# Reciprocals of the attention denominators: GpSimd's power of minus one in place of VectorE's reciprocal

## The chip, the cores and the metric

The kernel runs on one core of a Trainium2 chip. The time is the device time of one execution in microseconds (us). The core has five engines with queues of their own, which meet only through semaphores: TensorE (PE) multiplies matrices, VectorE (DVE) and ScalarE (ACT) work on tiles in SBUF and PSUM, GpSimd (POOL) on tiles in SBUF, and SyncE (SP) issues the DMAs here. PEld in the profile is PE's weight load, which runs beside its products.

## The reference

One token block of S = 2048 rows and D = 512 columns goes through a layernorm, and then through two branches whose results are added to the input.

```python
xn  = layernorm(x)
# A: linear attention, H = 32 heads of 16 columns
phi = lambda t: where(t > 0, t + 1, exp(t)) + 1e-6
pq, pk = phi(q), phi(k)
kv  = einsum("bhsd,bhse->bhde", pk, v);  z = sum over s of pk
num = einsum("bhqd,bhde->bhqe", pq, kv)
den = einsum("bhqd,bhd->bhq", pq, z)[..., None] + 1e-6
A   = (num / den) @ wo
# B: gated feed-forward, F = 1792
B   = (silu(xn @ w_gate) * (xn @ w_up)) @ w_down
out = x + A + B
```

For each of the 2048 rows there are 32 denominators, one per head. The division by them is what the change touches.

## The kernel before

The rows are cut into NT = 16 tiles of 128 (the partitions). A small planner, `_Program`, takes operations in the order in which they are written, with the keys that they read and write. It gives each engine its own queue in that order, and puts a semaphore wait wherever an operation depends on one of another engine, or reads what an earlier one of its own engine wrote (PE excepted). So the order on every engine is that of the source, and an operation that waits holds back all that stands behind it on its engine.

The first 75 us do the layernorm, q, k and phi, the sum over k, and the feed-forward branch for the first 512 rows. The change is used after that.

**The F loop** (L1132, 14 chunks, `fc`) computes the feed-forward branch's hidden values for the other 1536 rows, in two halves `q`. Blocks of the product are combined so that seven products (`prod`, L846) take the place of eight, from sums of the weights that DVE forms (`w_sums`, L808, half of them in each chunk) and sums of the results (`u4`, L874, and `up22`, which writes the tile c, L879, both on DVE). POOL multiplies two of the four results of a chunk by the gate (`h22`, L883), DVE the two others (`h21`, L889). ACT does the gate (L868) and copies. Between the products `fill` puts matrix products of the first output tiles.

**The denominators** are worked off beside this, one tile `t` in each chunk 0 to 10 (`DIV`), in the order of the list `ORDER`, with two buffers each for `pz`, `den` and `rden`:

- `pz_mul` (L638, POOL): pq times z, 128x512, and a seventeenth column per head that holds 1e-6;
- `den_sum` (L644, DVE): the sum over the 17 columns of each head, which gives `den`, 128x32;
- `den_turn` (L650): `rden`, the reciprocals, 128x32;
- `pq_mul` (L654, POOL): pq times rden, spread over the 16 columns of a head;
- `turn` (L660, SP): a transposing DMA of pq into pk, from where PE reads it as weights for the output.

In a chunk the order is: `den_turn` after the two `u4`, then `up22` and `h22`, then `h21`, `w_sums`, `pq_mul` (which is also made to wait for the last weight sum), `turn`, `pz_mul` for the tile two further on (`pz_ahead`), and `den_sum` for the next chunk's tile. In chunks 9 and 10 POOL also scales half of M (L794), in 11 to 13 it copies parts of the down projection's weights (L998).

**The pair stage** (L1231) computes the output for the other 12 row tiles, in pairs, again with seven products for eight (`dprod`, L1083), and the attention's part (`attn`, L1089). DVE forms the sums of hidden values (`h_sum`, L1067), and the results (L1103, L1109, L1115). The five last denominators are worked off here (`DIV2`), one in each of the pairs 1 to 4 and the last one late in pair 4. There `den_sum`, `den_turn`, `pq_mul` and `turn` follow each other directly.

Of the kernel before, what the change touches and what calls it, by code (L numbers as in the profile page):

```python
# [7 lines left out]
ALU = mybir.AluOpType  # L8

P = 128  # L10
# [11 lines left out]
NH = D // DH  # L22
# [95 lines left out]
def bass_parallel_sum__linear_attn_block__swiglu_ffn__prompt_kernel(nc, A_x, A_wqkv, A_wo, B_x, B_w_gate, B_w_up, B_w_down, out):  # L118
    xin = A_x[0]
    oview = out[0]  # L120
    K = _Program()
    bf, f32 = dt.bfloat16, dt.float32

    with contextlib.ExitStack() as es:
        E = es.enter_context

        def sb(name, shape, dtype):
            return E(nc.sbuf_tensor(name, shape, dtype))
# [29 lines left out]
        den = sb("den", [P, 2, NH], f32)  # L158
        rden = sb("rden", [P, 2, NH], f32)
        out_sb = sb("out_sb", [P, 2, D], bf)  # L160
        ident = sb("ident", [P, P], bf)
        maskt = sb("maskt", [P, P], bf)
        eps5 = sb("eps5", [P, 1], f32)
        stats = sb("stats", [P, NT, 6], f32)
        mv = sb("mv", [P, NT, 2], f32)
        lnv = sb("lnv", [P, NT], f32)
# [99 lines left out]
        for t in range(4, 16):  # L266
            xload("sp", t)

        K.add("pool", lambda e: e.memset(eps5[:, :], 1e-5), w=[("eps5",)])
        K.add("pool", lambda e: e.memset(ident[:, :], 0.0), w=[("ident",)])  # L270
        K.add("pool", lambda e: e.affine_select(
            out=ident[:, :], in_=ident[:, :], compare_op=ALU.not_equal, fill=1.0,
            base=0, pattern=[[-1, P]], channel_multiplier=1), r=[("ident",)], w=[("ident",)])
# [373 lines left out]

        def den_turn(t):
            i = SLOT[t] % 2
            K.add("dve", lambda e: e.reciprocal(rden[:, i, :], den[:, i, :]), r=[("den", i)], w=[("rden", i)])  # L650

        def pq_mul(t, after=()):
            i = SLOT[t] % 2
# [10 lines left out]
        def divide(t):  # L664
            den_sum(t)
            den_turn(t)
            pq_mul(t)
            turn(t)
            pz_mul(t + 2)
# [462 lines left out]
        for fc in range(NFC):  # L1132
# [16 lines left out]
            if fc in DIV:  # L1149
                den_turn(DIV[fc])  # L1150
# [80 lines left out]
        for p in range(NP2 - 1):  # L1231
# [6 lines left out]
            if p == 0:  # L1238
                t_sum(3, 0)
                t_sum(3, 1)  # L1240
                h_sum(0, 2)
            else:
                copies(p, 0)
                if p > 1:
                    h_sum(p, 3)
                den_sum(t)
                den_turn(t)
                pq_mul(t)
                turn(t)
# [104 lines left out]
```

## Time and profile before

| | |
|---|---|
| median of 3 runs | 200.51 us (200.5 to 200.74) |
| profiled execution, its own time | 200.89 us |
| its span in the profile | 199.6 us |
| granted clock of TensorE | 1.00 |
| busy: PE, DVE, ACT, POOL | 98%, 85%, 77%, 61% |

The span runs from the first to the last instruction that the profile records. "Busy" counts instructions that run; PE's ends are modelled, since matrix products overlap. A row of a group names the line of the source, engine, operation, the tile written and the tiles read, shapes and count, then the busy time in us with the mean of one in ns, then the idle time of the engine just before them and what ended it. A line of the timeline gives start and length in us, and in brackets the idle time ahead of it with its releaser. The profile calls the tile c22 "c", p5 "p", and sil4 "zacc", the buffer that it lies in; hT, xn and pq also hold hidden values later on.

### The profile page before, as it was taken

Reading aid. Unit: us, or ns where it says so; the run is one execution under the profiler, and the core shown is the slowest. Engines: PE = TensorE matmul, PEld = TensorE weight load, DVE = VectorE, ACT = ScalarE, POOL = GpSimd, SP = SyncE. Lnnn points to the kernel's source line nnn. Section 1 sums busy time; section 2 is a strip of 40 time slices with the busy share of each in tenths; the row PEclk is TensorE's granted clock in tenths of the full one; section 3 lists DMA queues with packets and bytes.
Section 4 is the critical chain, followed back from the end, with each engine's and each line's share of the span. In section 5 each row is a group of like instructions: output and inputs, shape, how many; then the busy total and the mean of one; then the engine's idle time right before and its main releaser. Section 6 shows DMA issues by size and latency. Waiting matters only on the chain.

```text
span 199.6 us, 3566 instructions
## 1 busy us (share of the span) xinstructions
PE 195.1 (98%) x1193; PEld 114.8 (58%) x1207; DVE 170.5 (85%) x339; ACT 153.6 (77%) x308; POOL 122.3 (61%) x150
## 2 busy tenths in 40 slices
PE   8899999999999999999999999999999999999995
PEld 2344444444544445555555555555555888888884
DVE  2999998894797798988888998887799999998866
ACT  3799887749889988689898988888989968475200
POOL 3687876799995544787677666768877004413220
DMA  6943243289990000011111221000210012132223
GB/s 180 355 122 81 57 87 73 50 282 364 375 295 3 0 3 0 0 28 31 26 26 26 53 56 23 4 0 7 45 34 0 3 39 66 30 79 66 45 69 118
DMA packets 28899, 15.97 MB, mean 80 GB/s; under 512 B 17232, under 2 KB 28880, under 8 KB 28880
## 3 DMA queue, kind: packets, MB, share of 16 engines
q1 hardware_dynamic: 28320, 15.28, 27.3%
q10 hardware_dynamic: 560, 0.46, 0.7%
q8 instruction: 9, 0.15, 0.3%
q14 instruction: 10, 0.08, 0.1%
HBM read 9.70 MB, written 2.10 MB: 59 GB/s over the span
## 4 chain that ended last, share of the span: by engine, by line
PE 94%; DVE 2%; DMA 2%; issue 1%; ACT 0%; POOL 0%; SPq 0%
PE pb L846 32%; PE pb L1083 16%; PE pb L431 13%; PE pb L556 12%; PE pb L480 7%; PE pb L682 6%; PE pb L1089 5%; PE pb L686 2%; DMA x_sb<-in_A_x_dram 2%; PE pb L605 1%; PE pb L674 0%; DVE pq L470 0%; PE pb L398 0%; POOL ef L459 0%; DVE stats L298 0%
## 5 line engine op out<-in xcount | busy, mean ns | idle before, releaser
L654 POOL TENSOR_TENSOR pq<-pq,rden 128x512 bf16<-128x512 bf16 x16 | 16.9, 1056 | 36.7 <-DVE rden L650 23.1
L868 ACT ACTIVATE zacc<-pb,iw 128x384 bf16<-128x384 f32 x56 | 31.3, 590 | 5.9 <-PE pb L846 4.7
L431 PE MATMUL pb<-wqkv,xnT 128*128 128x512 bf16 x110 | 25.1, 379 | 0.2
L846 PE MATMUL pb<-xnT,wg 128*128 128x384 bf16 x112 | 25.1, 326 | 0.0
L638 POOL TENSOR_TENSOR pz<-pq,zbc 128x512 f32<-128x512 bf16 x16 | 18.6, 1164 | 5.3 <-DVE ef L808 3.8
L883 POOL TENSOR_TENSOR hT<-c,zacc 128x384 bf16<-128x384 f32 x18 | 16.1, 915 | 6.0 <-DVE c L879 4.0
L459 POOL TENSOR_SCALAR ef<-ef 128x512 bf16<-128x512 bf16 x25 | 15.5, 620 | 5.8 <-ACT ef L452 5.6
L879 DVE TENSOR_TENSOR c<-pb,p 128x384 f32<-128x384 f32 x28 | 15.5, 555 | 4.1 <-PE pb L846 2.8
L431 PEld LDWEIGHTS pb<-wqkv,xnT 128*128 128x128 bf16 x112 | 10.9, 98 | 13.3 <-DVE pk L470 0.4
L452 ACT ACTIVATE ef<-pb 128x512 bf16<-128x512 f32 x25 | 14.8, 593 | 3.9 <-PE pb L431 3.9
L874 DVE TENSOR_TENSOR pb<-pb,p 128x384 f32<-128x384 f32 x28 | 15.3, 561 | 1.7 <-PE pb L846 0.9
L497 POOL TENSOR_TENSOR zacc<-zacc,pk 128x512 f32<-128x512 f32 x13 | 15.4, 1181 | 1.0
L856 ACT ACTIVATE pb<-pb 128x384 f32<-128x384 f32 x28 | 12.7, 473 | 3.8 <-PE pb L846 2.9
L846 PEld LDWEIGHTS pb<-xnT,wg 128*128 128x128 bf16 x112 | 10.6, 98 | 7.7 <-ACT pb L856 0.8
L556 PE MATMUL pb<-xnT,wg 128*128 128x512 bf16 x56 | 14.7, 379 | 0.0
L556 PE MATMUL pb<-xnT,wu 128*128 128x512 bf16 x53 | 14.3, 379 | 0.1
L846 PE MATMUL pb<-xnT,wqkv 128*128 128x384 bf16 x56 | 13.7, 326 | 0.0
L846 PE MATMUL pb<-GT,wqkv 128*128 128x384 f16 x56 | 13.7, 326 | 0.0
L846 PE MATMUL pb<-wo,wqkv 128*128 128x384 f16 x56 | 13.7, 326 | 0.0
L298 DVE BATCH_NORM_STATS2 stats<-x_sb 128x6 f32<-128x512 bf16 x16 | 10.8, 678 | 3.0 <-DMA x_sb<-in_A_x_dram 3.0
L1089 PE MATMUL pb<-M,pk 128*128 128x256 bf16 x96 | 13.4, 273 | 0.0
L480 PE MATMUL pb<-pk,xn 128*128 128x512 bf16 x55 | 12.5, 379 | 0.1
(210 smaller groups left out, 488.6 us busy)
## 6 DMA issues: line engine op xcount, KB each, us to landing
x_sb<-in_A_x_dram SPq DMA_DIRECT2D x14, 128.0 KB, 4.5
wg<-in_B_w_gate_dram SPq DMA_DIRECT2D x2, 896.0 KB, 8.3
wu<-in_B_w_up_dram SPq DMA_DIRECT2D x2, 896.0 KB, 9.6
wd<-in_B_w_down_dram SPq DMA_DIRECT2D x2, 896.0 KB, 13.7
out_dram<-out_sb SPq DMA_DIRECT2D x24, 64.0 KB, 1.6
wqkv<-in_A_wqkv_dram SPq DMA_DIRECT2D x3, 256.0 KB, 5.0
wqkv<-in_A_wqkv_dram SPq DMA_DIRECT2D x1, 512.0 KB, 9.0
wo<-in_A_wo_dram SPq DMA_DIRECT2D x1, 512.0 KB, 10.0
```

Of the source, the lines that this page charges most:

```text
L431: K.add("pe", [(lambda e, c=c: e.matmul(banks[b][:, :], src[:, c, t * P:(t + 1) * P], wqkv[:, c, col:col + D], start=(c == 0), stop=(c == ...
L459: K.add("pool", lambda e: e.tensor_scalar(out=buf, in0=buf, scalar1=top, scalar2=0.0, op0=ALU.min, op1=ALU.max), r=[bkey] + tkeys, w=[bkey])
L480: K.add("pe", [(lambda e, c=c: e.matmul(banks[c][:, :], src[:, t, c * P:(c + 1) * P], pk[:, t, :], start=first, stop=last)) for c in range ...
L556: fns.append(lambda e, c=c, b=b, w_=w_: e.matmul(banks[b][:, :], w_[:, c, fc * P:(fc + 1) * P], xnT[:, c, C * 512:(C + 1) * 512], start=(c ...
L638: K.add("pool", lambda e: e.tensor_tensor(out=pzh[i][:, :, 0:DH], in0=heads(pq[:, t, :]), in1=heads(zbc[:, :]), op=ALU.mult), r=[("pq", t) ...
L654: K.add("pool", lambda e: e.tensor_tensor(out=heads(pq[:, t, :]), in0=heads(pq[:, t, :]), in1=rden[:, i, :][:, :, None].broadcast_to([P, N ...
L846: K.add("pe", [(lambda e, c=c: e.matmul(banks[bank][:, 0:TS], L[i][:, c, :], R[i][:, c, ts], start=(start and c == 0), stop=(c == 1), skip ...
L868: K.add("act", lambda e: e.activation(sil4[:, n, :], bk(bank), ACT.Silu, scale=iw[:, 0:1]), r=[B(bank), ("iw",)], w=[("sil4", n), ("zacc", ...
L879: K.add("dve", lambda e: e.tensor_tensor(out=c22[:, q, :], in0=bk(b), in1=p5[:, q, :], op=ALU.add), r=[B(b), ("p5", q)], w=[("c22", q)])
L883: K.add("pool", lambda e: e.tensor_tensor(out=hj(fc)[:, TB + q * TS:TB + (q + 1) * TS], in0=c22[:, q, :], in1=sil4[:, 2 * q + 1, :], op=AL ...
L1083: K.add("pe", [(lambda e, k=k: e.matmul(split(banks[b][:, 0:HD]), L[:, k, :], cut[:, :, k * P:(k + 1) * P], start=(start and k == 0), stop ...
L1089: K.add("pe", [(lambda e, g=g: e.matmul(dk(b), pk[:, SLOT[t], g * P:(g + 1) * P], M[:, g, lo:lo + HD], start=False, stop=(g == NG - 1), sk ...
```

## The change

The reciprocal `den_turn` moves from DVE to POOL. POOL computes it as `den` to the power of `minus`, a tile of 128x32 that holds -1 and is written once by a memset on POOL near the start, between the memset of `ident` and the selection that makes it the identity. The calls of `den_turn` stay where they are, so that the new instruction stands in POOL's queue ahead of the chunk's two `h22`; in the pair stage it stands right ahead of `pq_mul`.

```diff
         eps5 = sb("eps5", [P, 1], f32)
+        minus = sb("minus", [P, NH], f32)
...
         K.add("pool", lambda e: e.memset(ident[:, :], 0.0), w=[("ident",)])
+        K.add("pool", lambda e: e.memset(minus[:, :], -1.0), w=[("minus",)])
...
         def den_turn(t):
             i = SLOT[t] % 2
-            K.add("dve", lambda e: e.reciprocal(rden[:, i, :], den[:, i, :]), r=[("den", i)], w=[("rden", i)])
+            K.add("pool", lambda e: e.tensor_tensor(
+                out=rden[:, i, :], in0=den[:, i, :], in1=minus[:, :], op=ALU.pow), r=[("den", i), ("minus",)], w=[("rden", i)])
```

## The prediction

> **What bounds the kernel now.** I read the page's shares and its chain first.
>
> ```profile
> PE 195.1 (98%) x1193; PEld 114.8 (58%) x1207; DVE 170.5 (85%) x339; ACT 153.6 (77%) x308; POOL 122.3 (61%) x150
> ...
> PE 94%; DVE 2%; DMA 2%; issue 1%; ACT 0%; POOL 0%; SPq 0%
> ```
>
> TensorE (PE) carries the time; neither VectorE (DVE) nor GpSimd (POOL) stands in the chain. The change touches only the stretch from 75 us on, so I asked for busy time by stretch: seven chunks of the F loop (L1132), the rest of that loop, the pair stage (L1231 and after).
>
> ```profile
> 91.39:130.32 38.93, 38.72 (x224) 21.62 (x227) 34.44 (x72) 34.74 (x70) 27.74 (x29) 1.00 0.13 30
> 130.32:153.80 23.48, 23.38 (x135) 13.05 (x136) 19.98 (x38) 20.89 (x39) 18.57 (x19) 1.00 0.09 18
> 153.80:197.40 43.60, 43.60 (x395) 37.91 (x393) 39.03 (x78) 24.11 (x34) 9.84 (x10) 1.00 0.20 53
> ```
>
> The columns are the stretch, its length, and the busy time (with instructions) of PE, PE's weight loads, DVE, ACT and POOL, then clock and DMA. PE is busy 38.72 + 23.38 + 43.60 = 105.70 us of 106.01. At most 0.3 us can be won there, whatever DVE is spared; what can happen is a loss. So the question is how long POOL may be kept before PE hears of it. Seven chunks take 38.93 us, 5.56 us each. One chunk of POOL, from its timeline:
>
> ```profile
> 96.87 1.79 POOL L883 TENSOR_TENSOR hT<-c,zacc 128x384 bf16<-128x384 f32 x2 [0.65 <-DVE c L879]
> 99.63 1.06 POOL L654 TENSOR_TENSOR pq<-pq,rden 128x512 bf16<-128x512 bf16 x1 [0.97 <-DVE wqkv L808]
> 100.64 1.17 POOL L638 TENSOR_TENSOR pz<-pq,zbc 128x512 f32<-128x512 bf16 x1
> 102.50 1.78 POOL L883 TENSOR_TENSOR hT<-c,zacc 128x384 bf16<-128x384 f32 x2 [0.69 <-DVE c L879]
> ```
>
> Two products h22, a wait for DVE's weight sums (L808), pq_mul, pz_mul, a wait for c. The new instruction goes in the last gap, ahead of h22. The gaps are 0.69 and 0.97 us.
>
> **The change, part by part.** Removed: 16 reciprocals on DVE.
>
> ```profile
> L650 DVE RECIPROCAL rden<-den 128x32 f32<-128x32 f32 x16 | 5.5, 345 | 0.2
> L644 DVE TENSOR_REDUCE den<-pz 128x32 f32<-128x544 f32 x16 | 11.4, 710 | 0.0
> ```
>
> That frees 16 x 0.345 = 5.5 us of DVE. In a chunk it buys nothing: the reciprocal runs 101.26 to 101.60, and the next DVE instruction, c (L879), starts at 101.86 after 0.26 us of waiting for PE. Without the reciprocal DVE only waits longer. I count 0, at most the 0.3 us above. pq_mul comes no earlier either: it waits for the weight sums.
>
> Added once: a memset of 128x32 on POOL. The rows bound it by 98 ns (memset 128x1) and 204 ns (128x128). It delays the identity, ready at 1.57 us and first read by PE at 4.34 us: 0; without that cover 0.2 us at most.
>
> Added waits: den_sum two tokens on must wait until POOL has read den (two chunks of room), and pq_mul for POOL's own result. Behind pq_mul stand pz_mul, then DVE's den_sum. In the loop h22 lies between, so it is free; in the pair stage it is direct. The only POOL instruction that waits for POOL now (L271) sits idle 0.24 us, against 0.09 us from reciprocal to pq_mul: +0.15 us.
>
> Added 16 times: the power on 128x32, of which **the trace shows no row**. Bounds: below, an ordinary POOL pass. Two-input f32 passes take 915 ns for 384 columns and 1181 for 512, 2.08 ns a column; with the 190 ns of a 128x1 instruction, 32 columns cost 0.26 us. Scaling that column by what a reciprocal costs DVE against a plain pass, (343 - 155)/31 = 6.1 ns against (555 - 155)/384 = 1.04, nearly 6 times, gives 0.19 + 32 x 2.08 x 6 = 0.6 us. Above: POOL computes a power in steps. TENSOR_SCALAR with two steps takes 620 ns for 512 columns and 1120 for 1024, 0.98 ns a column, 0.49 a step. No row says how many steps a power has; I assume 70, for a logarithm, a product and an exponential, and 200 as the far end: 0.19 + 32 x 70 x 0.49 ns = 1.29 us, and 3.3 us. **I take 1.3 us**, with 0.26 and 3.3 as ends. The row nearest in work is DVE's reciprocal (0.6 by scaling), but a power of a variable exponent is more than a division, so I go to twice that.
>
> Now the room for C, the power's time. With C below 0.69 nothing in a chunk moves. Above, h22 moves later by C - 0.69, and ends at 98.66 + (C - 0.69); the first weight sum on DVE starts at 98.80. What then happens is in the trace of DVE, at a chunk where h22 was late (142.15 to 143.93):
>
> ```profile
> 132.24 0.41 DVE L808 TENSOR_TENSOR wqkv<-wg,wu 128x512 f16<-128x512 bf16 x1
> ...
> 143.50 0.72 DVE L808 TENSOR_TENSOR wqkv<-wg,wu 128x512 f16<-128x512 bf16 x1
> ```
>
> The same sum took 0.41 us alone and 0.72 beside h22, ending 0.29 us after it; the other overlapped one (87.69) took 0.67 and ended 0.28 after. So h22 holds the sums back, the sums hold pq_mul, and POOL's loop closes: C, h22 1.79, h22's end to pq_mul 0.69 (88.08 to 88.77), pq_mul to pz_mul 1.01, pz_mul to the next 1.12 (85.17 to 86.29): 4.61 + C. It fits 5.56 up to C = 0.95. The sums sit ahead of den_sum and u4 (L874) on DVE; u4 for the first half ends at 100.70, PE wants its bank at 101.01, so 0.3 us of delay reach PE.
>
> The rule behind this is in the Trainium skill, "SBUF — State Buffer", section "Who interferes with whom": a DVE instruction with two SBUF inputs and a GpSimd instruction that reads SBUF exclude each other for the whole instruction. The 0.72 agrees. Without such a rule the loop would be 3.92 + C, it would fit up to C = 1.64, and the loop's part of the sum below would be 0.
>
> Sum at C = 1.3. Each chunk is 4.61 + 1.3 - 5.56 = 0.35 us too long. Chunks 1 to 8: 2.8. In chunks 9 and 10 POOL also scales M (L794, 1.12 us each; the step to the next is 1.1): 0.35 + 1.1 = 1.45 each, of which I count one, because chunk 11 has no power and POOL waits 1.38 + 0.50 us in it. Chunk 0 is free: den is ready at 79.57 and POOL idles until 80.45 and again 0.84 us later. Less what is absorbed: u4's 0.3 and the 0.3 of DVE freed: -0.6. Loop: 2.8 + 1.45 - 0.6 = +3.65 us.
>
> Pair stage, five powers. At pair 1 den_sum ends at 164.75; pq_mul, now 165.22 to 166.28, becomes about 166.2 to 167.3 with C and the wait on itself. A sum of L1067 with two SBUF inputs wants to start at 166.60, and PE waits for it already (PEld idle 0.19 us at 167.27): about +0.3. At pairs 2 and 3 such a sum lies behind pz_mul (1.30 us instead of 0.61 at 173.79), so it ends up to 0.7 us later, or earlier if it slips in between: +0.1 each. At pair 4, 0. The last power has the 2.6 us until pq_mul, which waits for a sum of L1067 until 191.32; its transpose lands 2.4 us after 192.40, and PE reads it from 196.00. Hidden. Together +0.5.
>
> Total +4.15 us on the profiled execution: 200.89 (span 199.6, 1.3 around it) becomes 205.0. On the median shown, 200.51, it is **204.7 us**.
>
> **The rivals.** 0.2% is 0.4 us, about what a measurement of this kernel can tell from no change.
> - **Hidden: not slower.** POOL is the place and C the price, 0.95 us the point that decides. With C at 0.6 h22 and the sums stay where they are, the pair stage shifts pq_mul by 0.4 us to 166.7 at most, and the time is 200.5 (200.2 to 200.9). For it: 0.6 is the scaled reciprocal, POOL is 61% busy. Against: nothing here shows POOL computing more than two simple steps a column. Chance 0.28, with 0.02 more that the power is not run on POOL as said (then the DVE row of 0.345 comes back, 200.5).
> - **POOL becomes the bound.** C above 2 us: POOL never idles, so chunks 9 and 10 both count with their 1.1. At C = 3 that is 2.05 x 10 + 2.2 - 0.6 = +22 us in the loop, and some 2 in the pair stage (pq_mul there 2.7 later, against sums that PE waits for): 224.5. At C = 2 it is 1.05 x 10 + 2.2 - 0.6 + 0.9 = +13: 213.5; at 3.3, 228. For it: a power in unrolled software can be long. Chance 0.29.
> - **DVE's relief counts.** PE's 0.3 us of gaps from 91 us on and the 0.2 at 167.27 go, and a little ahead of 91: 200.0. Against: DVE waits for PE behind the reciprocal. Chance 0.05.
>
> **How the numbers follow.** The forecast (C from 0.95 to 2, that is 201 to 213.5) has 0.36 and gives 204.7. Its part, the hidden case and the lower part of the long power (to C = 2.85, 223) make the range, 200.2 to 223; left out are the relief's 0.05 and some 0.12 above. Faster 0.05; within 0.2%, 0.30; slower 0.36 + 0.29 = 0.65.
>
> **What would show it.** The row of the new instruction on POOL: below 0.95 us the forecast falls, above 2 it is too small. In the chunks: h22 (L883) starting right behind the power with no idle time, L808 sums of 0.7 us instead of 0.42, chunks of 5.9 us instead of 5.56, PE waiting for u4. At pair 1, PE waiting longer for L1067. What would make it wrong besides C: DVE's sums going ahead of a late h22. POOL's own loop is then 1.79 + 1.01 + 1.12 + C = 3.92 + C, which fits 5.56 up to C = 1.64, and C = 1.3 costs only the pair stage's 0.5: 201.0, inside the forecast's span.

## The result and the profile after

The changed kernel takes 254.04 us (median of 6, 253.43 to 255.37) against 200.57 us before (6 runs beside it): 1.267 times as long, 95% interval 1.2645 to 1.2692. The forecast was 204.7 us, the range ended at 223.

The page of the changed kernel: the shares, the clock granted to TensorE by slices, and the chain that ended last.

```profile
PE 212.5 (84%) x1193; PEld 116.9 (46%) x1207; DVE 171.8 (68%) x323; ACT 155.8 (62%) x308; POOL 211.0 (84%) x167
...
PEclk9999999999999995897979887979859999999997
...
POOL 50%; PE 34%; issue 7%; DVE 5%; DMA 2%; ACT 1%; SPq 0%; POOLq 0%; DVEq 0%
...
L652 POOL TENSOR_TENSOR rden<-den,minus 128x32 f32<-128x32 f32 x16 | 88.6, 5540 | 11.1 <-DVE den L646 11.1
```

The last row is the new instruction: 16 of them, 88.6 us, 5.54 us each, where the reciprocal took 0.345 us on VectorE. POOL now makes half of the chain, and 33% of the span lies on this one line. One chunk of the F loop in POOL's timeline (start, length):

```profile
108.83 5.61 POOL L652 TENSOR_TENSOR rden<-den,minus 128x32 f32<-128x32 f32 x1
114.41 1.77 POOL L886 TENSOR_TENSOR hT<-c,zacc 128x384 bf16<-128x384 f32 x2
116.15 1.05 POOL L657 TENSOR_TENSOR pq<-pq,rden 128x512 bf16<-128x512 bf16 x1
117.16 1.15 POOL L640 TENSOR_TENSOR pz<-pq,zbc 128x512 f32<-128x512 bf16 x1
118.28 5.65 POOL L652 TENSOR_TENSOR rden<-den,minus 128x32 f32<-128x32 f32 x1
```

No idle time is left: from power to power 9.45 us, against 5.56 for a chunk before. That is the power and the 3.9 us of the four others. How it reaches PE stands in the table of waits (who waits for whom: us in total, times, longest):

```profile
PEld pb L849 <- DVE c L882: 37.5, 24, 4.3
ACT zacc L871 <- POOL hT L886: 33.0, 18, 5.6
DVE c L882 <- POOL hT L886: 30.1, 18, 4.7
PE pb L849 <- DVE c L882: 26.1, 19, 3.8
...
PE pb L1092 <- DMA pk<-pq: 6.8, 3, 3.6
```

The gate and c have one buffer for each half. ACT and DVE may not write the next chunk's values until h22 has read the last ones, and PE waits for c to have its PSUM bank. PEld and PE wait for the same thing there, so the two are not added. The last line is the pair stage: PE waits for the transposed quotients.

Where the 52.6 us between the spans (252.2 and 199.6) arose, from the starts of the first h22 of each chunk: until chunk 0's h22 4.3 (84.71 against 80.45), from there to chunk 11's 39.7 (101.44 against 61.70), to chunk 13's -0.4, from there to the end 9.0 (55.5 against 46.4).

### The profile page after: what moved, and what is told of

It reads as the page before. It is cut to its first block, busy times and chain, and to the rows that moved or that the text cites. A ratio compares the mean times of both kernels' runs of the same rounds, so it can differ in the third digit from the quotient of the medians.

```text
span 252.2 us, 3578 instructions
## 1 busy us (share of the span) xinstructions
PE 212.5 (84%) x1193; PEld 116.9 (46%) x1207; DVE 171.8 (68%) x323; ACT 155.8 (62%) x308; POOL 211.0 (84%) x167
## 4 chain that ended last, share of the span: by engine, by line
POOL 50%; PE 34%; issue 7%; DVE 5%; DMA 2%; ACT 1%; SPq 0%; POOLq 0%; DVEq 0%
POOL rden L652 33%; PE pb L433 10%; PE pb L558 9%; POOL pz L640 6%; PE pb L849 6%; POOL pq L657 5%; PE pb L482 5%; POOL hT L886 3%; DVE xnT L1070 1%; PE pb L685 1%; DMA x_sb<-in_A_x_dram 1%; DMA pk<-pq 1%; DVE out_sb L1118 1%; POOL xn L886 1%; PE pb L1092 1%
## 5 line engine op out<-in xcount | busy, mean ns | idle before, releaser
L652 POOL TENSOR_TENSOR rden<-den,minus 128x32 f32<-128x32 f32 x16 | 88.6, 5540 | 11.1 <-DVE den L646 11.1
L871 ACT ACTIVATE zacc<-pb,iw 128x384 bf16<-128x384 f32 x56 | 31.9, 585 | 45.3 <-POOL hT L886 33.0
L849 PE MATMUL pb<-wqkv,wu 128*128 128x384 f16 x56 | 16.4, 389 | 26.2 <-DVE c L882 26.1
L849 PE MATMUL pb<-xnT,wg 128*128 128x384 bf16 x112 | 31.2, 390 | 0.0
L849 PEld LDWEIGHTS pb<-wqkv,wu 128*128 128x128 bf16 x56 | 3.6, 101 | 38.3 <-DVE c L882 37.5
L849 PEld LDWEIGHTS pb<-xnT,wg 128*128 128x128 bf16 x112 | 12.7, 116 | 11.8 <-issue 5.7
L849 PE MATMUL pb<-ef,wqkv 128*128 128x384 f16 x56 | 15.3, 408 | 0.0
L849 PE MATMUL pb<-GT,wqkv 128*128 128x384 f16 x56 | 14.5, 342 | 0.0
```

What stands on the lines that cost most here:

```text
L652: K.add("pool", lambda e: e.tensor_tensor(out=rden[:, i, :], in0=den[:, i, :], in1=minus[:, :], op=ALU.pow), r=[("den", i), ("minus",)], w ...
L849: K.add("pe", [(lambda e, c=c: e.matmul(banks[bank][:, 0:TS], L[i][:, c, :], R[i][:, c, ts], start=(start and c == 0), stop=(c == 1), skip ...
L871: K.add("act", lambda e: e.activation(sil4[:, n, :], bk(bank), ACT.Silu, scale=iw[:, 0:1]), r=[B(bank), ("iw",)], w=[("sil4", n), ("zacc", ...
```

## Experiments

Theory A: the loss is the price of the power on GpSimd, which fills its queue. Rival B: it is the move (new waits, one engine doing three steps in order). All kernels differ from the changed one only as shown, and in what that needs (where VectorE inverts a part, `pq_mul` waits for that part too); the times before, beside them, were 200.54 to 200.65 us.

**The same move with a cheap instruction.** The multiplication stands in the power's place, so the division is left out.

```diff
-                out=rden[:, i, :], in0=den[:, i, :], in1=minus[:, :], op=ALU.pow), ...
+                out=rden[:, i, :], in0=den[:, i, :], in1=minus[:, :], op=ALU.mult), ...
```

> The same move, the same place in GpSimd's queue, the same waits, but the instruction multiplies den by -1 instead of raising it to the power of -1 (so the division is left out of the computation). Theory A, the price of the power itself on GpSimd: the instruction takes about 0.26 us, fits the 0.69 us gap ahead of h22, the chunks stay at 5.56 us, the time is 200.5 us (200.2 to 201.0). Rival B, the move itself, that is the new chain den on VectorE, den_turn and pq_mul on GpSimd and what stands behind them: most of the 53 us stay, over 225 us.

Measured 201.09 us, ratio 1.002 (1.0005 to 1.0034). The group of the instruction in this run:

```profile
L652 POOL TENSOR_TENSOR rden<-den,minus 128x32 f32<-128x32 f32 x16 | 4.4, 275 | 24.5 <-DVE den L646 24.5
```

0.275 us, as an ordinary pass was reckoned (0.26), and the move costs at most 0.3% (the time lies 0.1 us above A's 201.0). B falls. VectorE was spared all 16 reciprocals here as well, and nothing was won.

**Which stage.** Two kernels, each with the power in one stage and VectorE's reciprocal in the other.

```diff
         def den_turn(t):
             i = SLOT[t] % 2
+            if SLOT[t] < 11:       # the other kernel: SLOT[t] >= 11
+                K.add("dve", lambda e: e.reciprocal(rden[:, i, :], den[:, i, :]), r=[("den", i)], w=[("rden", i)])
+                return
```

> Power on GpSimd for the last five tiles only (pair stage); VectorE's reciprocal for the eleven of the F loop. Theory A: the F loop is as before at full clock. From the last h22 to the end the changed kernel took 55.5 us against 46.4 before, 9 us more, because the transposed quotients come late; so 209.5 us (207 to 211). Rival C, the pair stage's loss is only an echo of the loop's (work that lagged, a lower clock): 201 to 203 us.

> Power on GpSimd for the eleven tiles of the F loop, VectorE's reciprocal for the last five. Theory A: GpSimd is full in the loop, chunks of 3.92 + 5.5 = 9.4 us; 254.0 less the pair stage's 9 = 245 us (243 to 247), and the granted clock still falls in the loop. Rival C: 251 us or more.

Measured 209.42 us (1.0439, 1.0422 to 1.0457) and 244.79 us (1.2202, 1.2173 to 1.2231): +8.8 and +44.1, together 52.9 of the 53.5. The stages add up, and each comes out as it was read from the starts of h22, so C falls.

**The price by width.** First half of the columns, then eight widths in one kernel, each in other tiles, executed once. VectorE inverts the rest.

```diff
+            n = NH // 2            # the other kernel: n = (32, 1, 2, 4, 8, 12, 16, 24, 32, 8, 8, 4, 8, 16, 2, 1)[SLOT[t]]
+            K.add("dve", lambda e: e.reciprocal(rden[:, i, n:], den[:, i, n:]), r=[("den", i)], w=[("rden", i, 1)])
             K.add("pool", lambda e: e.tensor_tensor(
-                out=rden[:, i, :], in0=den[:, i, :], in1=minus[:, :], op=ALU.pow), ...
+                out=rden[:, i, 0:n], in0=den[:, i, 0:n], in1=minus[:, 0:n], op=ALU.pow), ...
```

> The power on 16 of the 32 columns, VectorE's reciprocal on the other 16, everything else as in the changed kernel. Theory A1, the price goes by columns: 0.19 + 16 x (5.5 - 0.19)/32 = 2.85 us, chunks of 3.92 + 2.85 = 6.8 us against 5.56, ten of them +12, the two scalings of M +2, chunk 0 and the pair stage +3: some 217 us (212 to 221). Rival A2, the price is fixed (dispatch, loading of code): the instruction still takes about 5.5 us and the time is 250 us or more.

> One look at the price by width: the power on 1, 2, 4, 8, 12, 16, 24 and 32 columns in different tiles, VectorE's reciprocal on the rest. From 32 columns (5.43 us) and 16 (2.9 to 3.1 in the half-width run): theory A1, a straight line of 0.155 us a column with 0.45 us at none, so 1 column 0.6, 4 columns 1.1, 8 columns 1.7, 24 columns 4.2 us. Rival A3, columns are worked off in blocks (of 16 or 8): the same price for 1 to 8 columns, steps above.

The half-width kernel took 218.48 us (1.0889, 1.0868 to 1.0911), its power 3.0 us, as A1 reckoned; A2 falls. The groups of the kernel with eight widths:

```profile
L655 POOL TENSOR_TENSOR rden<-den,minus 128x32 f32<-128x32 f32 x2 | 11.1, 5530 | 1.2 <-DVE den L646 1.2
...
L655 POOL TENSOR_TENSOR rden<-den,minus 128x16 f32<-128x16 f32 x2 | 5.8, 2898 | 3.0 <-DVE den L646 3.0
L655 POOL TENSOR_TENSOR rden<-den,minus 128x24 f32<-128x24 f32 x1 | 4.2, 4161 | 0.0
L655 POOL TENSOR_TENSOR rden<-den,minus 128x12 f32<-128x12 f32 x1 | 2.3, 2267 | 0.0
L655 POOL TENSOR_TENSOR rden<-den,minus 128x4 f32<-128x4 f32 x2 | 2.0, 1010 | 9.9 <-DVE den L646 9.9
L655 POOL TENSOR_TENSOR rden<-den,minus 128x1 f32<-128x1 f32 x2 | 1.6, 794 | 1.0 <-DVE den L646 1.0
L655 POOL TENSOR_TENSOR rden<-den,minus 128x2 f32<-128x2 f32 x2 | 1.4, 698 | 1.2 <-DVE den L646 1.2
```

A straight line from 2 columns on: (4161 - 698)/22 = 157 ns a column, 0.38 us at none. No steps, so A3 falls. One column costs more than two, 0.79 us against 0.70; why stays open. The first power of the changed kernel's profiled execution took 5.45 us, like the later ones.

**The exponent.**

```diff
-        K.add("pool", lambda e: e.memset(minus[:, :], -1.0), w=[("minus",)])
+        for k, v in enumerate((-1.0, 1.0, 2.0, 0.5)):
+            K.add("pool", lambda e, k=k, v=v: e.memset(minus[:, k, :], v), w=[("minus", k)])
...
-                out=rden[:, i, :], in0=den[:, i, :], in1=minus[:, :], op=ALU.pow), ...
+                out=rden[:, i, :], in0=den[:, i, :], in1=minus[:, SLOT[t] % 4, :], op=ALU.pow), ...
```

> Does the price hang on the exponent? Tiles take turns with exponents -1, 1, 2 and 0.5 (so that only every fourth tile gets its reciprocal). Theory F, one routine for all: 5.4 to 5.7 us for each, 254 us in all. Rival G, -1 goes a long way and simple exponents have a short one: three of four instructions well under 5 us, and a time under 240 us.

254.45 us in one execution. The 16 instructions took 5.43 to 5.80 us, and the first four of the pair stage, one for each exponent, 5.43 us each. F holds.

**What the prediction's loop is worth at the price that it assumed.** With 6 columns the power takes 1.32 us, nearly the 1.3 of the forecast; 8 take 1.63. The edit is that above with n = 6 and n = 8.

> Power on 6 columns, VectorE on 26; by the line 1.4 us. Theory D, a late h22 lets the weight sums go ahead, so GpSimd's own loop 3.92 + C decides: 5.3 us fits the chunk of 5.56, only the pair stage costs: 200.9 to 201.8 us. Rival E, the prediction's step (h22 holds the sums back through the shared read port, they hold pq_mul, loop of 4.61 + C): 6.0 us a chunk, 0.45 too long, ten chunks and one scaling of M: 204.5 to 206 us.

> Power on 8 columns, VectorE on 24; by the line 1.7 us. Theory D: 3.92 + 1.7 = 5.62 against 5.56, still no loss to speak of in chunks 1 to 8, the scalings of M add a lag that the room of some 3 us (time until the next chunk needs the buffers) takes: 201 to 202.5 us. Rival E: 4.61 + 1.7 = 6.3, 0.75 too long: 207 to 209 us.

Measured 206.66 us (1.0298, 1.028 to 1.0316) and 206.42 (1.0289, 1.0271 to 1.0306). The first is rival E, just above its numbers; D falls there. A chunk of it, on POOL and on DVE:

```profile
104.08 1.32 POOL L655 TENSOR_TENSOR rden<-den,minus 128x6 f32<-128x6 f32 x1
105.37 1.78 POOL L889 TENSOR_TENSOR hT<-c,zacc 128x384 bf16<-128x384 f32 x2
107.97 1.05 POOL L660 TENSOR_TENSOR pq<-pq,rden 128x512 bf16<-128x512 bf16 x1 [0.82 <-DVE wqkv L814]
```

```profile
106.23 1.20 DVE L814 TENSOR_TENSOR wqkv<-wu 128x512 f16<-128x512 bf16 x1
107.47 0.42 DVE L814 TENSOR_TENSOR wqkv<-wqkv,wg 128x512 f16<-128x512 f16 x1
```

The sum that takes 0.42 us alone takes 1.20 and ends 0.28 us after h22 (107.43 against 107.15); pq_mul waits for the sums. From chunk 1 to 9 a chunk is 5.89 us (47.13/8; single ones take 5.59 to 6.03), 4.61 + 1.32 = 5.93 by the prediction's loop. PE's weight load waits 9.0 us for u4 in 12 waits, against 1.1 in 4 before: the path that the prediction named.

With 8 columns the time lies between the numbers of the two theories, and each holds for a part of the loop. In the first chunks (93.76, 99.30, 104.87, 110.40: 5.55 each) the sums come ahead of h22, while POOL is still at the power:

```profile
103.27 1.65 POOL L655 TENSOR_TENSOR rden<-den,minus 128x8 f32<-128x8 f32 x1
104.87 1.84 POOL L889 TENSOR_TENSOR hT<-c,zacc 128x384 bf16<-128x384 f32 x2
```

```profile
104.19 0.41 DVE L814 TENSOR_TENSOR wqkv<-wu 128x512 f16<-128x512 bf16 x1
104.64 0.42 DVE L814 TENSOR_TENSOR wqkv<-wqkv,wg 128x512 f16<-128x512 f16 x1
```

From 116 us on h22 has slipped under the sums (one takes 1.13 at 123.28), and chunks take 6.05 to 6.07. So a longer power cost no more than a shorter one: which of the two loops holds hangs on which side of h22 the sums fall.

**The power behind h22.** In the F loop the power moves behind both h22 in POOL's queue, where it fills the wait for the sums; with 6 and with all 32 columns.

```diff
             if fc in DIV:
-                den_turn(DIV[fc])
+                turn_dve(DIV[fc])
...
                 h22(q, fc)
+            if fc in DIV:
+                turn_pool(DIV[fc])
```

> The six-column run (206.7 us, chunks of 5.97 us) with one thing moved: in the F loop the power stands behind the two h22 in GpSimd's queue instead of ahead of them. Theory E, the loss there came from h22 being pushed onto the weight sums: with h22 on time and the power in the wait for the sums (the power itself did not hold up such sums in the trace), GpSimd's loop is 3.92 + 1.32 = 5.24 and fits 5.56: 200.8 to 202 us. Rival H, it is simply too much work on GpSimd or on the chain from den to pq_mul: 205 to 207 us as before the move.

> The changed kernel with all 32 columns, the power again behind the two h22. Theory A, at 5.5 us GpSimd is full wherever the power stands: chunks of 3.92 + 5.5 = 9.4 us, 252 to 256 us. Rival I, the place ahead of h22 is what costs, since the gate and c wait for h22: under 240 us.

With 6 columns 203.69 us (1.0144, 1.0119 to 1.017), between the two expectations. By the starts of h22, chunks 1 to 9 take 44.4 us, 5.55 each, against 47.1 with the power ahead of h22 and 44.0 before: most of the loop's loss is gone, as E said, and H falls. What stays, 3.1 us in the medians and 2.3 between the spans of the profiled executions, was not in E's reckoning. The largest part, 1.25 us, arises in chunks 9 and 10, where POOL also scales M: they take 6.4 and 6.6 us against 6.0 and 5.8. With 32 columns 254.56 us (1.2683, 1.2641 to 1.2725): the place does not matter once POOL is full. I falls.

**The pair stage.** Power for the first two tiles (15 and 6) alone, shown against the kernel with the pair stage's powers; then the same with their transposing DMAs moved in SyncE's queue.

```diff
-            if SLOT[t] < 11:
+            if SLOT[t] not in (11, 12):
...
                 pq_mul(t)
-                turn(t)
+                if p > 2:
+                    turn(t)
...
             dout(p, 1, 0, b)
+            if p in (1, 2):
+                turn(t)
```

> Power on GpSimd only for the first two tiles of the pair stage (15 and 6), all other reciprocals on VectorE. Their quotients are read two pairs, some 14 us, later. Theory J, the pair stage's 9 us come from the last three tiles, whose transposes PE waits for: 200.5 to 201.5 us here, no gain and no loss. Rival K, each of the five powers costs its share: 200.6 + 2 x 1.8 = 204 us.

> The run with powers for tiles 15 and 6 only (202.3 us), with their transposing DMAs written behind the last store of their pair instead of right behind pq_mul. Theory M: the loss of that run came from SyncE's queue, where the transpose waited for the late pq_mul until 171.55 us and held back the stores behind it (next one 173.51 instead of 167.54), so that the result buffers stayed full, VectorE waited 2.6 us for them and TensorE 1.6 for VectorE. Then this is 200.5 to 201.2 us. Rival K, GpSimd's work itself or the lateness of the quotients: 202 us or more as before.

The first took 202.27 us (1.008, 1.0055 to 1.0105). Neither J nor K: there is a loss, but PE waits for no transpose. SyncE's timeline before and in this run, and DVE's timeline and PE's waits in this run, show another way:

```profile
166.30 1.20 SPq L660 DMA_TRANSPOSE pk<-pq  x1
167.54 3.62 SPq L692 DMA_DIRECT2D out_dram<-out_sb  x4
```

```profile
171.55 1.91 SPq L666 DMA_TRANSPOSE pk<-pq  x1
173.51 2.00 SPq L698 DMA_DIRECT2D out_dram<-out_sb  x4
```

```profile
175.30 0.48 DVE L1121 SCALAR_TENSOR_TENSOR out_sb<-pb,iso,x_sb 128x256 bf16<-128x256 f32 x1 [2.11 <-DMA out_dram<-out_sb]
```

```profile
PEld pb L1089 <- DVE out_sb L1121: 1.6, 1, 1.6
PE pb L1089 <- DVE out_sb L1121: 1.3, 1, 1.3
```

The transpose stands in SyncE's queue and waits for pq_mul, which comes late. Four stores stand behind it. They leave at 173.51 us instead of 167.54, the result buffers stay full, DVE waits for them 2.1 us and PE for DVE. With the transposes behind the stores the time is 200.68 us, ratio 1.0001 (0.999 to 1.0012): theory M holds, and two powers of 5.4 us are then hidden. That kernel is no better than the one before; none of them is.

## Why the prediction was wrong, point by point

- **What bounds the kernel, and that nothing can be won: right.** The multiplication in the same place spares VectorE everything and gives 1.002.
- **The price of the power: wrong, and this is the step that failed.** "No row says how many steps a power has; I assume 70 [...] and 200 as the far end": 1.29 and 3.3 us, taken 1.3. Measured 5.4 to 5.8. At the 0.49 ns of a step that the text used, the 157 ns of a column are 320 steps; that a step costs half of what two cost, no row shows either. The far end was no bound from any row, only a second guess beside the first, and the range hung on it.
- **Scaling by VectorE's reciprocal: wrong kind of row.** It gave 0.6 us, a ninth. VectorE's reciprocal costs nearly 6 plain columns, GpSimd's power 75 (157 ns against 2.08): the factor did not carry over from one engine to the other.
- **The room and the loop of 4.61 + C: right for the price assumed** (the 6-column run: 5.89 us a chunk for 5.93). The sum for it was short, 204.7 against 206.66, because chunk 0 was counted as free; it and the way to chunk 1, where POOL has no gap ahead of h22 before, cost 1.8 us (88.12 against 86.29). Two terms came near: 3.1 us from chunk 1 to 9 for 2.8, and 0.6 behind the loop for 0.5. Two errors partly cancel, which is luck: chunks 9 and 10 cost 0.6 for 1.45, and chunks 11 and 12 give back 0.2 where 0.6 had been taken off. Half of that 0.6 was VectorE's relief, which can't show in a run where VectorE still inverts 26 columns.
- **The rival "POOL becomes the bound": right kind, wrong loop.** With C = 5.5 chunks take 9.45 us, which is 3.92 + C and not 4.61 + C. The sums then lie beside the power, long before h22, and nothing waits for them. The last paragraph had named this as what could go wrong. By 4.61 + C ten chunks would have lost 45.5 us, by 3.92 + C 38.6; 39.7 were measured, with the scalings of M.
- **The pair stage: mechanisms missed.** The text looked at the sums of L1067 behind POOL, and counted the last power as hidden. In the changed kernel POOL waits for no other engine from the start of the first of the five powers (208.40) to the end of the last pq_mul (245.80), so the last quotients come late. Their transpose and PE's reading of them, before (timeline) and after (the chain that ended last):

```profile
192.40 1.21 SPq L660 DMA_TRANSPOSE pk<-pq  x1
196.00 1.47 PE L1089 MATMUL pb<-M,pk 128*128 128x256 bf16 x12
```

```profile
245.83 2.40 DMA pk<-pq
248.28 1.69 PE pb L1092 x12
```

From the start of the last h22, PE reads them after 51.5 us (248.28 less 196.74) where it took 42.8 (196.00 less 153.18): 8.7 of the stage's 9.0 us. PE's waits for transposes (5.2 us in the pair-only run) lie inside that and are not added. What SyncE's queue adds, where a late transpose holds back stores, is shown for two powers alone (1.7 us); its share in the 8.8 us is not. The transpose in front of the stores stands in the code, and the text did not ask who stands behind it.

- **A DVE sum beside POOL: right for h22, not for the power.** The Trainium skill, "SBUF — State Buffer", section "Who interferes with whom", lets an instruction of GpSimd that reads SBUF and one of VectorE with two SBUF inputs exclude each other to the end. Beside h22 that fits (1.20 us, ending 0.28 us after it). Beside the power it doesn't, and there the measurement decides: in the changed kernel these sums run in the midst of a power from 208.40 to 213.83 at their usual 0.61 us.

```profile
210.16 0.61 DVE L1070 TENSOR_TENSOR xnT<-ef,xnT 128x896 f16<-128x896 bf16 x1
210.69 0.62 DVE L1070 TENSOR_TENSOR xn<-wqkv,xnT 128x896 f16<-128x896 bf16 x1
...
211.62 0.62 DVE L1070 TENSOR_TENSOR xnT<-xn,wqkv 128x896 f16<-128x896 f16 x1
```

## What to carry to other kernels

A price that no row shows is the whole forecast where it decides: bound it by the point from which it matters, and let the range run as far as the operation could go, not as far as a guess of its length. Before an engine with spare time takes a new instruction, compare the instruction with the room in one turn of its queue, and look at which side of it the neighbours fall; the same work one place further back cost half as much here (six columns, 3.1 us for 6.1). And where a result comes later, follow it into the DMA queue: what waits there in order is late as well.

## What the runs showed of the hardware

- GpSimd's power, with exponent -1, costs 157 ns a column of 128 partitions and 0.38 us besides, from 2 columns on. At 32 columns it takes 5.4 to 5.8 us for exponents -1, 1, 2 and 0.5 alike; a multiplication of 32 columns costs 0.275 us in the same place.
- PE's granted clock was 1.00 throughout before. In the changed kernel it fell in the F loop, where PE waits up to 3.8 us at a time: 0.82 from 114.41 to 123.91 us, 0.934 over the span. A faster PE could not have shortened that stretch, since POOL was busy for 9.50 of its 9.50 us. In the profiled half-width run the clock stayed at 1.00, though PE waits in that loop too, 1.7 us at the longest.
- In the pair stage a lower clock does cost time, where PE is the last to finish. In the profiled pair-only execution (210.64 us) the granted clock was 0.77 from 202.0 us on, and the last 12 products took 2.74 us instead of 1.47. The two executions of that kernel with a clock of 1.00 took 209.26 and 209.30 us.
